# Hash logits of fourteen heads in four products instead of six, their low part in rows of its own

## The chip, the cores and the metric

The kernel runs on one core of a Trainium2 chip. The metric is the time of one execution on the device in microseconds (us): three runs of the kernel before took 732.75, 733.07 and 733.6 us, median 733.07 us.

## The reference

Two stages follow one another. First, attention with a hash mask for 2 batches x 8 heads (16 heads), 768 tokens, 64 numbers per head: q and k are multiplied by a 64 x 6 projection, the signs of the six products are a token's bucket, and a query sees only keys of its own bucket.

```python
q_bits = (np.einsum('bhsd,dk->bhsk', q, proj) > 0).astype(np.int64)
k_bits = (np.einsum('bhsd,dk->bhsk', k, proj) > 0).astype(np.int64)
mask = q_bucket[:, :, :, None] == k_bucket[:, :, None, :]
scores = np.where(mask, scale * np.matmul(q, k.transpose(0, 1, 3, 2)), -1000000000.0)
attn = softmax(scores); attn_out = np.matmul(attn, v)
```

Then the 1536 x 512 result goes through two dense layers of the form `act(x @ w_in) @ w_out` with 2048 hidden units each. The change touches the attention alone.

## The kernel before, in words

All matrix products run on TensorE in fp32r, each operand split into a rounded high part and a low part, so that one product of fp32 operands becomes two or three matmuls. Tensors named `...h` and `...l` (or `_hi`, `_lo`) are such parts. The order on every engine is the order in which the program is written (`manual_schedule`): each engine works through its own list, and waits only for data and for buffers.

The attention is a loop over 96 steps (16 heads of six query tiles of 128 rows). A step does, in the order of the string `ORDER = "ACaBbETQPR"`: A and B, three transposes each of a finished score tile into the PSUM tile `pt` (L658), of which ScalarE copies the high part `pth` (L665); C, the `clamp` of this step's scores (VectorE, L610); a and b, the low parts `ptl` (VectorE, L670); E, the exponential (ScalarE, L621); T, whatever was filed for this step in the table `todo` by `at(step, function)`; Q, the score products of the next step (L598), first `kh` with `qx`, then `kb` with `qb`, which holds the mask; P and R, the products with v (L682, L683). The PSUM pool `ps_t` has three buffers that `pt` tiles and the hash logits' tile `prep` take in turn, so the second transposes of a step take the buffer of the first transposes of the step before, and wait for that buffer's `ptl`.

Each head n is prepared about two heads ahead by `prep(n)`, which returns small functions that `start_prep` files. For n > 1: `s0` (GpSimd) rounds and subtracts q, and sends the rounded q to the upper half of `qx` by a DMA (L473 to L477); `s1` (GpSimd) does the same for k: `kh` (a `pcopy`, L109), and its low part in `qk_m` (L481). `s2` computes the hash logits: for each half of 384 tokens three matmuls, `qk_m`, `kh` and `qx` against columns of the projection's parts `pwt` (L492), all six into one PSUM tile, and right behind them `s2m`, one VectorE instruction that turns logits into mask rows `mk` (L512: greater than zero, times a constant). `s4` sends the low operands into `qb` and `kb` (L517, L518), and `s5`, one step after `s2`, sends `mk` into them in four DMAs of 32 rows (L526). `start_prep(n+1)` and `s2` of head n stand in the same step, the GpSimd part of head n+1 first. All those DMAs are issued by SyncE (SP), whose list is in program order too, with the loads of q and k (L379, L392) and the exchange of normalisers through `scr` (L647, L653).

Heads 0 and 1 are prepared at the start by other functions. In the first steps GpSimd also zeroes rows of `qb` and `kb` (`zero_rows`, step 1). Beside the preparation GpSimd has the attention outputs (`x_out` L707 to L714, `x_split` L718 and L719) and, from step 70 on, operands of the dense layers.

Of the kernel before, what the change touches and what calls it, by code (L numbers as in the profile page):

```python
# [12 lines left out]
F32 = mybir.dt.float32  # L13
# [4 lines left out]
ALU = mybir.AluOpType  # L18
# [10 lines left out]


def mask_consts():
    c = np.zeros((64, 2), np.float32)
    c[12:18, 0] = -3.0e38
    c[0:18, 1] = 1.0
    c[38:44, 0] = -3.0e38
    c[32:38, 1] = -2.0 * CBIG
    c[38:50, 1] = CBIG
    return np.concatenate([c, c])


# [1 line left out]
def lsh_attention_moe_kernel(  # L42
# [8 lines left out]
):  # L51
    nc = tc.nc
    B, H, D, S = qt.shape
    NTOK, DM = out.shape
    P = 128
    NT = S // P
# [294 lines left out]
    def attention():  # L351
        with ExitStack() as es:
# [18 lines left out]
            def load_q(n):  # L371
                b, h = head(n)
                t = nat.tile([P, S], F32, tag="qn", name="qn")
                if n == 0:
                    for f in range(2):
                        c = slice(f * HS, (f + 1) * HS)
                        nc.sync.dma_start(t[0:D, c], qt[b, h, 0:D, c])
                else:
                    nc.sync.dma_start(t[0:D], qt[b, h])  # L379
                nat_t["q", n] = t  # L380

            def load_k(n):
# [27 lines left out]
            mc = cst.tile([P, 2], F32, name="mc")  # L410
            load_q(1)
            load_k(1)
            load_v(0)
# [28 lines left out]
            pr = pp.tile([P, 2, NB], F32R, tag="p", name="pr")  # L442

            def pcol(j, o):
                w = pw[:, j, o : o + 2 * NB * (2 if o else 1)]
                return w.rearrange("p (a b) -> p a b", a=2)[:, :, 0:NB]

            def prep_w():
                nc.gpsimd.tensor_copy(mc, pc[:, 2 * NB : NC])
                pcopy(pr, pjt)  # L450
                nc.gpsimd.tensor_sub(pcol(2, 0)[0:D], rnd(pr[0:D]), pjt[0:D])
                pcopy(pcol(2, 32)[D:P], rnd(pr[D:P]))
                nc.gpsimd.tensor_sub(pcol(1, 32)[D:P], pjt[D:P], rnd(pr[D:P]))
                pcopy(pcol(1, 32)[0:D], rnd(pr[0:D]))
                nc.scalar.mul(pcol(0, 0), rnd(pr), -1.0)

            opnd = {}

            def prep(n):
# [10 lines left out]
                opnd[n] = (kh, qx, qb, kb, vv_box)  # L470

                def s0():
                    nc.gpsimd.tensor_scalar(qk_m[0:D], qn[0:D], QSCALE, 1.0, ALU.mult, ALU.mult)  # L473
                    nc.sync.dma_start(rnd(qx[D:P]), rnd(qk_m[0:D]))
                    if n > 1:
                        nc.gpsimd.tensor_scalar(qn[0:D], qn[0:D], QSCALE, 1.0, ALU.mult, ALU.mult)
                        nc.gpsimd.tensor_sub(qx[0:D], qn[0:D], rnd(qk_m[0:D]))  # L477

                def s1():
                    pcopy(kh, kn)  # L480
                    nc.gpsimd.tensor_sub(qk_m[D:P], kn[D:P], rnd(kh[D:P]))  # L481

                def second():
# [15 lines left out]

                def s2():  # L500
                    pt = ps_t.tile([P, 512], F32, tag="pt", name="prep")
                    logits(pt, 0, 64, True, False)
                    logits(pt, 1, 0, False, True)
                    mk_box.append(pt)
                    if n > 1:
                        s2m()

                def s2m():
                    pt = mk_box.pop()
                    mk = hd.tile([P, HS], F32, tag="mk", name="mk", bufs=1)  # L510
                    mk_box.append(mk)
                    nc.vector.tensor_scalar(  # L512
                        mk, pt[:, :HS], mc[:, 0:1], mc[:, 1:2], ALU.is_gt, ALU.mult
                    )

                def s4():
                    nc.sync.dma_start(rnd(qb[D:P]), rnd(qk_m[0:D]))  # L517
                    nc.sync.dma_start(rnd(kb[D:P]), rnd(qk_m[D:P]))  # L518

                def s5():  # L520
                    mk = mk_box.pop()
                    for f in range(2):
                        c = slice(f * HS, (f + 1) * HS)
                        rows = (qb, f * D), (kb, f * D + 32)
                        for t, r in rows[::-1] if f else rows:
                            nc.sync.dma_start(rnd(t[0:32, c]), mk[r : r + 32])  # L526

                def first(q1, k1):
                    cs2 = [slice(f * HS, (f + 1) * HS) for f in range(2)]
# [45 lines left out]
                return s0, s1, s2, s3, s4, s5  # L575

            NSTEP = NHD * NT
            p_t = {}
# [158 lines left out]
            NZL = 2  # L737
            PVLAG = LAG + 1
            todo = {}

            def at(step, f, *args):
                todo.setdefault(step, []).append((f, args))
# [3 lines left out]

            at(1, first_v)
            at(1, zero_rows)

            for f, st in zip(second[3:7], (2, 7, 1, 3)):  # L750
                at(st, f)

            def start_prep(n):
                b0 = NT * (n - 2)
                s0, s1, s2, s3, s4, s5 = prep(n)
                s0()
                s1()
                for f, early, late in ((s2, 8, 8), (s3, 11, 6), (s4, 6, 5), (s5, 9, 9)):
                    at(early if n == 2 else b0 + late, f)

            for u in range(NHD // 2 - 1):
                at(2 * NT * (u + 1) + XO - 3 * (u == NHD // 2 - 2), x_out, u)
# [40 lines left out]
            for i in range(NSTEP + PVLAG):  # L803
                if i == NSTEP:
                    es_s.close()
                    mps["h"] = ctx.enter_context(
                        tc.tile_pool(name="ps_h", bufs=1, space=PSUM, side="right")
                    )
                parts = iter(range(max(0, 2 * (i - NSTEP)), min(2 * (i - NSTEP) + 2, 2 * KD)))
                for part in parts:  # L810
                    r_in(0, part // KD, part % KD, part % KD + 1)
                    break
                kk = i - LAG
                tr = 0 <= kk < NSTEP
                g, j = divmod(kk, 3)
                kv = i - PVLAG
                gv, jv = divmod(kv, 3)
                for op in ORDER if i != 2 else ORDER.replace("TQ", "QT"):
                    if op == "A" and tr:
                        trp(g, 2 * j)  # L820
                    elif op == "B" and tr:
                        trp(g, 2 * j + 1)
                    elif op == "a" and tr:
                        trl(g, 2 * j)
                    elif op == "b" and tr:
                        trl(g, 2 * j + 1)
                    elif op == "C" and i < NSTEP:
                        clamp(i)
                        if i == 3:
                            second[7]()  # L830
                    elif op == "E" and i < NSTEP:
                        expo(i)
                    elif op == "Q" and i + 1 < NSTEP:
                        qk(i + 1, (0, 1) if i else (1,))
                        if i == 0:
                            keep_warm(4, 256)
                    elif op == "P" and 0 <= kv < NSTEP:
                        pv(gv, 2 * jv)
# [431 lines left out]
```

## Time and profile before

| what | value |
|---|---|
| runs | 732.75, 733.07, 733.6 us |
| span of the profiled execution | 731.7 us, 11216 instructions |
| time outside the span, against the median | 1.4 us |
| TensorE's granted clock | 0.997 of full speed on average |
| attention | from about 8 us to about 232 us of the span |
| DMA share in the attention | 0.5 to 0.7 of 16 engines |

A row of the page or of a timeline gives the engine, the line of the program, the operation, output and inputs by name, the shape, and then durations. PE is TensorE, PEld its weight loads, DVE VectorE, ACT ScalarE, POOL GpSimd, SPq the queue of DMA issues on SyncE. In a timeline the first number is the start in us, the second the time taken; a number in square brackets is how long the engine stood idle before it, and who ended that.

### The profile page before, as it was taken

The page shows a single profiled execution, that of the slowest core. Times are in us where ns is not written, and L with a number is a line of the kernel's source. Part 1 is how long each engine was busy: PE and PEld are TensorE (multiplying, and loading weights), DVE is VectorE, ACT ScalarE, POOL GpSimd, SP SyncE. Part 2 cuts the span into 40 slices and gives each one's busy share as a digit, 9 for nine tenths or more (in the row PEclk, how much of TensorE's full clock was granted, in tenths as well). Part 3 has the DMA queues.
Part 4 walks back from the last instruction along what each step waited for, and adds up shares of the span by engine and source line. Part 5 has one row for each costly group of instructions (what it writes and reads, how often), then busy time and mean ns, then how long its engine had stood idle before and what let it go on. Part 6 is the DMA issues. An engine that isn't in the chain of part 4 may idle for free.

```text
span 731.7 us, 11216 instructions
## 1 busy us (share of the span) xinstructions
PE 725.2 (99%) x3865; PEld 634.4 (87%) x3865; DVE 616.2 (84%) x1142; ACT 470.5 (64%) x965; POOL 184.9 (25%) x193
## 2 busy tenths in 40 slices
PE   8999999999999999999999999999999999999998
PEld 6999999999998788888888888888888888888886
DVE  7988889989988959888878797998699899897864
ACT  7888888888898765536546465676635556455340
POOL 6958778879894000000000000000000000000000
PEclk9999999999999999999999999999999999999999
DMA  5665565566624311122211221301302122211004
GB/s 150 167 160 146 159 179 154 155 165 166 186 74 130 98 59 58 57 72 74 87 58 58 87 84 60 116 0 59 114 2 80 65 71 73 87 58 57 1 1 172
DMA packets 25993, 69.53 MB, mean 95 GB/s; under 512 B 4464, under 2 KB 6992, under 8 KB 25936
## 3 DMA queue, kind: packets, MB, share of 16 engines
q1 hardware_dynamic: 25632, 68.62, 31.8%
q8 instruction: 30, 0.49, 0.3%
q14 instruction: 27, 0.22, 0.1%
q10 hardware_dynamic: 304, 0.20, 0.1%
HBM read 49.09 MB, written 3.19 MB: 71 GB/s over the span
## 4 chain that ended last, share of the span: by engine, by line
PE 94%; ACT 2%; DVE 2%; DMA 1%; issue 0%; ACTq 0%; DVEq 0%
PE y L929 36%; PE X L992 11%; PE s L598 9%; PE pt L658 8%; PE Y L992 8%; PE W L992 7%; PE u L683 4%; PE u L682 4%; PE h L346 4%; PE prep L492 2%; ACT p L621 1%; ACT pth L665 0%; DMA kn<-in_kt_dram 0%; DMA ul<-uh 0%; DVE gl L889 0%
## 5 line engine op out<-in xcount | busy, mean ns | idle before, releaser
L670 DVE TENSOR_TENSOR ptl<-pt,pth 128x384 fp32r<-128x384 f32 x192 | 98.1, 552 | 23.6 <-ACT pth L665 22.2
L665 ACT CAST pth<-pt 128x384 fp32r<-128x384 f32 x192 | 82.7, 482 | 28.9 <-PE pt L658 28.8
L621 ACT ACTIVATE p<-p,mn 128x768 f32<-128x768 f32 x96 | 90.9, 947 | 2.0 <-DVE p L610 1.9
L610 DVE TENSOR_SCALAR_CACHE_REDUCE p<-s 128x768 f32<-128x768 f32 x96 | 90.5, 944 | 1.0 <-PE s L598 1.0
L943 DVE TENSOR_TENSOR xq<-xq,y 128x512 f32<-128x512 f32 (+1 forms) x113 | 75.5, 678 | 13.8 <-PE y L929 13.0
L658 PE MATMUL pt<-ident,p 128*128 128x128 f32 x576 | 80.4, 274 | 0.1
L929 PE MATMUL y<-wh,gh 128*128 128x512 f32 (+1 forms) x194 | 75.4, 389 | 0.0
L929 PE MATMUL y<-wl,gh 128*128 128x512 f32 (+1 forms) x194 | 75.4, 389 | 0.0
L929 PE MATMUL y<-wh,gl 128*128 128x512 f32 (+1 forms) x194 | 75.2, 388 | 0.0
L929 PE MATMUL y<-gh,wh 128*128 128x512 f32 x192 | 75.1, 391 | 0.0
L929 PE MATMUL y<-gh,wl 128*128 128x512 f32 x192 | 75.0, 390 | 0.0
L929 PE MATMUL y<-gl,wh 128*128 128x512 f32 x192 | 74.8, 390 | 0.0
L259 ACT CAST wh<-wb 128x512 fp32r<-128x512 f32 x64 | 39.4, 619 | 54.7 <-DVE wb L246 26.2
L658 PEld LDWEIGHTS pt<-ident,p 128*128 128x128 f32 x576 | 68.4, 140 | 6.2 <-ACT p L621 0.7
L682 PE MATMUL u<-pth,vv 128*128 128x384 f32 x192 | 64.9, 338 | 0.0
L683 PE MATMUL u<-ptl,vv 128*128 128x384 f32 x192 | 64.8, 337 | 0.0
L598 PE MATMUL s<-kh,qx 128*128 128x384 f32 x192 | 56.0, 374 | 0.1
L598 PE MATMUL s<-kb,qb 128*128 128x384 f32 x192 | 50.0, 343 | 0.0
L261 DVE TENSOR_TENSOR wl<-wb,wh 128x512 fp32r<-128x512 f32 x62 | 42.2, 686 | 3.9 <-ACT wh L259 3.6
L943 DVE TENSOR_TENSOR yr<-yr,y 128x512 f32<-128x512 f32 x56 | 38.2, 683 | 7.8 <-PE y L929 6.9
L929 PEld LDWEIGHTS y<-wh,gl 128*128 128x128 f32 x194 | 36.4, 188 | 7.6
L929 PEld LDWEIGHTS y<-gl,wh 128*128 128x128 f32 x192 | 36.0, 188 | 7.9 <-DVE gl L889 0.3
(271 smaller groups left out, 1848.5 us busy)
## 6 DMA issues: line engine op xcount, KB each, us to landing
raw<-in_wt_dram SPq DMA_DIRECT2D x64, 512.0 KB
kn<-in_kt_dram SPq DMA_DIRECT2D x15, 384.0 KB
vn<-in_vt_dram SPq DMA_DIRECT2D x8, 384.0 KB
ul<-uh SPq DMA_DIRECT2D x16, 192.0 KB
rb<-scr SPq DMA_DIRECT2D x16, 192.0 KB
qn<-in_qt_dram SPq DMA_DIRECT2D x15, 192.0 KB
qx<-qk_m SPq DMA_DIRECT2D x15, 192.0 KB
qb<-qk_m SPq DMA_DIRECT2D x15, 192.0 KB
```

Source lines behind the costliest of these rows:

```text
L261: sub(lo, wf, rnd(hi))
L598: nc.tensor.matmul(s[:, f, :HS], a[:, c], bb[:, f * HS : (f + 1) * HS], start=st, stop=not st,)
L610: nc.vector.tensor_scalar(sb, s[:, :, :HS], NEG, None, ALU.min, ALU.min, accum_out=mn)
L621: nc.scalar.activation(p, p, AF.Exp, bias=mn, scale=-1.0, accum_out=z_t[n][:, t : t + 1],)
L658: nc.tensor.transpose(ptile[:, j * P : (j + 1) * P], p_t[3 * g + j][:, t * P : (t + 1) * P], ident,)
L665: nc.scalar.copy(hi, ptile[:, :HS])
L670: nc.vector.tensor_sub(lo, ptile[:, :HS], rnd(hi))
L682: nc.tensor.matmul(ut[:, :HS], vv[:, t, :], hi, start=(t == 0), stop=False)
L683: nc.tensor.matmul(ut[:, :HS], vv[:, t, :], lo, start=False, stop=(t == NT - 1))
L929: nc.tensor.matmul(y, w[:, js] if m == 0 else x[:, js], x if m == 0 else w[:, i0:i1], start=(n == 0), stop=(n == 5),)
L943: nc.vector.tensor_add(acc, acc, y)
L992: nc.tensor.matmul(bk[b], w[:, k], x, start=(first and i == 0), stop=(hook is not None and i == 2), skip_group_check=True,)
```

## The change

From the third head on (n > 1):

- `qx` is made by GpSimd on all 128 partitions (the q load brings q twice, 384 KB instead of 192 KB, as k already was), so the DMA of the rounded q goes. A new DMA sends `kh` into the lower half of `qk_m`, where the rounded q was; it waits for `kh`, GpSimd's fourth instruction of the head, where the old one waited for the first.
- The six logit matmuls become four: per half one of `qx` and one of `qk_m`, with a new weight tile `px` whose output has the logits of the high projection in rows 0 to 63 and those of its low part in rows 64 to 127. ScalarE copies the latter into `mk` right behind the matmuls.
- One step later, right behind that step's clamp, VectorE adds the former and then makes the mask rows, out of `mk` into `mk` (`mid`). `s5` follows in the same step as before, with four DMAs of 12 rows.
- `prep_x` builds `px` once, filed for step 2: on GpSimd a memset of 128 x 320 and three small copies, on SyncE two DMAs that wait for the memset and stand ahead of head 1's mask DMAs.

```diff
+            def prep_x():
+                nc.gpsimd.memset(rnd(px), 0.0)
...
+                pcopy(px[:, 0, q], rnd(pw[:, 0, 0 : 2 * NB]))
+                pcopy(px[0:D, 1, k], rnd(pw[0:D, 1, o : o + 2 * NB]))
+                pcopy(px[D:P, 1, k], rnd(pw[D:P, 2, o : o + 2 * NB]))
+                nc.sync.dma_start(rnd(px[D:P, 0, ql]), rnd(pw[0:D, 2, 0 : 2 * NB]))
+                nc.sync.dma_start(rnd(px[0:D, 1, kl]), rnd(pw[D:P, 1, o : o + 2 * NB]))
                 def s0():
+                    if n > 1:
+                        nc.gpsimd.tensor_scalar(qx, qn, QSCALE, 1.0, ALU.mult, ALU.mult)
+                        nc.gpsimd.tensor_scalar(qn[0:D], qn[0:D], QSCALE, 1.0, ALU.mult, ALU.mult)
+                        nc.gpsimd.tensor_sub(qx[0:D], qn[0:D], rnd(qx[0:D]))
+                        return
                 def s1():
                     pcopy(kh, kn)
+                    nc.sync.dma_start(rnd(qk_m[0:D]), rnd(kh[0:D]))
                     nc.gpsimd.tensor_sub(qk_m[D:P], kn[D:P], rnd(kh[D:P]))
                 def s2():
+                    if n > 1:
+                        for f in range(2):
+                            for j, x in enumerate((qx, qk_m)):
+                                nc.tensor.matmul(
+                                    pt[:, :HS],
+                                    px[:, j, 32 - 32 * f : 160 - 32 * f],
+                                    x[:, f * HS : (f + 1) * HS],
+                                    start=(f + j == 0),
+                                    stop=(f + j == 2),
+                                )
+                        mk = hd.tile([P, HS], F32, tag="mk", name="mk", bufs=1)
+                        mk_box.append(mk)
+                        nc.scalar.copy(mk[0:64], pt[64:128, :HS])
+                        return
                 def s2m():
                     if n > 1:
-                        s2m()
+                        pt, mk = mk_box
+                        del mk_box[0]
+                        nc.vector.tensor_add(mk[0:64], mk[0:64], pt[0:64, :HS])
+                        nc.vector.tensor_scalar(
+                            mk[0:64], mk[0:64], 0.0, mc[0:64, 2:3], ALU.is_gt, ALU.mult
+                        )
+                        return
                 def s5():
-                        rows = (qb, f * D), (kb, f * D + 32)
+                        rows = (qb, f * D, 0, 32), (kb, f * D + 32, 0, 32)
+                        if n > 1:
+                            rows = (qb, f * 32, 0, 12), (kb, f * 32 + 12, 6, 12)
+            at(2, prep_x)
+                mid.setdefault(9 if n == 2 else b0 + 9, []).append(s2m)
                     elif op == "C" and i < NSTEP:
                         clamp(i)
+                        for f in mid.pop(i, ()):
+                            f()
-    qt = q.transpose(0, 1, 3, 2)
+    qt = np.concatenate([q.transpose(0, 1, 3, 2)] * 2, axis=2)
```

## Rows read from the trace of the kernel before

**Rows 1.** Chain of work that ended last, 100 to 200 us: shares, then start, us, what

```profile
by line: PE s L598 31.1%; PE pt L658 29.9%; PE u L683 15.4%; PE u L682 15.4%; PE prep L492 7.4%; PE prep L640 0.9%
...
120.26 1.06 PE prep L492 x6
```

**Rows 2.** One head's stretch: us busy (instructions) of PE, PEld, DVE, ACT, POOL; clock, DMA

```profile
120.26:133.88 13.62, 13.62 (x92) 13.27 (x92) 12.11 (x27) 11.56 (x28) 8.91 (x10) 1.00 0.65 176
```

**Rows 3.** Instructions of the tile prep: count, min/median/max ns, first and last start, shapes

```profile
L492 PE MATMUL prep<-kh,pwt x30: 331/334/338, 13.2 to 202.5; 128*128 128x384 f32 x30
...
L512 DVE TENSOR_SCALAR mk<-prep,mc x15: 662/669/676, 14.3 to 203.3; 128x384 f32<-128x384 f32 x15
```

**Rows 4.** Groups by line: busy us, mean ns of one, idle before and what ended it

```profile
L670 DVE TENSOR_TENSOR ptl<-pt,pth 128x384 fp32r<-128x384 f32 x192 | 98.1, 552 | 23.6 <-ACT pth L665 22.2
...
L694 ACT COPY uh<-u 128x384 f32<-128x384 f32 x32 | 15.2, 475 | 0.0
```

**Rows 5.** Timeline from one head's logits to its first use of the mask

```profile
120.01 0.42 PE L492 MATMUL prep<-qk_m,pwt 128*128 128x384 f32 x1
...
122.06 0.95 DVE L610 TENSOR_SCALAR_CACHE_REDUCE p<-s 128x768 f32<-128x768 f32 x1
...
123.07 0.86 ACT L665 CAST pth<-pt 128x384 fp32r<-128x384 f32 x2 [1.27 <-PE pt L658]
...
123.59 1.02 DVE L670 TENSOR_TENSOR ptl<-pt,pth 128x384 fp32r<-128x384 f32 x2 [0.57 <-ACT pth L665]
...
124.61 0.82 PE L658 MATMUL pt<-ident,p 128*128 128x128 f32 x6
...
127.80 0.51 PE L598 MATMUL s<-kb,qb 128*128 128x384 f32 x2
```

**Rows 6.** VectorE instructions from SBUF to SBUF, by line

```profile
L539 DVE TENSOR_SCALAR qk_m<-qn x2: 351/352/352, 3.2 to 5.1; 64x384 fp32r<-64x384 f32 x2
...
L238 DVE TENSOR_SCALAR raw<-raw x5: 380/423/1085, 115.1 to 231.9; 128x512 uint32<-128x512 uint32 x5
...
L243 DVE SCALAR_TENSOR_TENSOR wb<-wb,raw x6: 681/693/1645, 142.3 to 235.3; 128x512 uint32<-128x512 uint32 x6
```

**Rows 7.** Timeline: one of them beside a GpSimd instruction

```profile
173.94 0.83 POOL L109 TENSOR_SCALAR kh<-kn 128x768 fp32r<-128x768 f32 x1
...
173.97 1.08 DVE L238 TENSOR_SCALAR raw<-raw 128x512 uint32<-128x512 uint32 x1
```

**Rows 8.** Timeline of GpSimd, some 3.2 us after the logits of heads 2, 8 and 15

```profile
27.51 0.84 POOL L109 TENSOR_SCALAR kh<-kn 128x768 fp32r<-128x768 f32 x1
...
109.47 1.85 POOL L707 TENSOR_TENSOR ul<-ul,uh 128x768 f32<-128x768 f32 x1
...
204.15 1.28 POOL L301 TENSOR_TENSOR t2l<-xq,t2h 128x512 fp32r<-128x512 f32 x1
```

**Rows 9.** Timelines of SyncE's DMA issues, and a GpSimd instruction that waits for one

```profile
115.58 0.29 SPq L647 DMA_DIRECT2D scr<-zt  x1
...
117.38 0.53 SPq L653 DMA_DIRECT2D rb<-scr  x1
...
122.77 1.22 SPq L526 DMA_DIRECT2D kb<-mk  x2
...
126.50 0.60 SPq L379 DMA_DIRECT2D qn<-in_qt_dram  x1
...
130.31 0.82 POOL L473 TENSOR_SCALAR qk_m<-qn 64x768 fp32r<-64x768 f32 x1 [0.97 <-DMA qn<-in_qt_dram]
```

**Rows 10.** Timelines of the start: GpSimd, then SyncE's queue, then PE

```profile
1.25 0.47 POOL L438 MEMSET wzero<- 128x448 f32 x1
...
14.53 0.82 POOL L109 TENSOR_SCALAR qb<-zero 32x768 fp32r<-32x768 f32 x1
...
15.02 0.58 SPq L526 DMA_DIRECT2D qb<-mk  x1
...
18.75 0.52 PE L598 MATMUL s<-kb,qb 128*128 128x384 f32 x2
```

More of the change, by code (lines that the diff above doesn't have):

```diff
@@ L31, in mask_consts @@
 def mask_consts():
-    c = np.zeros((64, 2), np.float32)
+    c = np.zeros((64, 3), np.float32)
     c[12:18, 0] = -3.0e38
     c[0:18, 1] = 1.0
-    c[38:44, 0] = -3.0e38
-    c[32:38, 1] = -2.0 * CBIG
-    c[38:50, 1] = CBIG
+    c[32:38, 0] = -3.0e38
+    c[32:50, 1] = CBIG
+    c[38:44, 1] = -2.0 * CBIG
+    for r in (0, 32):
+        c[r : r + 12, 2] = 1.0
+        c[r + 12 : r + 18, 2] = -2.0 * CBIG
+        c[r + 18 : r + 24, 2] = CBIG
     return np.concatenate([c, c])
@@ L53, in lsh_attention_moe_kernel @@
     B, H, D, S = qt.shape
+    D //= 2
     NTOK, DM = out.shape
@@ L378, in load_q @@
                 else:
-                    nc.sync.dma_start(t[0:D], qt[b, h])
+                    nc.sync.dma_start(t, qt[b, h])
                 nat_t["q", n] = t
@@ L409, in attention @@
             load_k(0)
-            mc = cst.tile([P, 2], F32, name="mc")
+            mc = cst.tile([P, 3], F32, name="mc")
             load_q(1)
@@ L444, in pcol @@
             def pcol(j, o):
-                w = pw[:, j, o : o + 2 * NB * (2 if o else 1)]
-                return w.rearrange("p (a b) -> p a b", a=2)[:, :, 0:NB]
+                o += NB if o else 0
+                return pw[:, j, o : o + 2 * NB].rearrange("p (a b) -> p a b", a=2)
             def prep_w():
@@ L455, in prep_w @@
                 nc.scalar.mul(pcol(0, 0), rnd(pr), -1.0)
+            px = wo[0].tile([P, DM], F32R, tag="ol1", name="px")[:, 0:320]
+            px = px.rearrange("p (a b) -> p a b", a=2)
+            def prep_x():
+                nc.gpsimd.memset(rnd(px), 0.0)
+                o = 32 + NB
+                q, k = slice(32, 32 + 2 * NB), slice(32 + 2 * NB, 32 + 4 * NB)
+                ql, kl = slice(96, 96 + 2 * NB), slice(96 + 2 * NB, 96 + 4 * NB)
+                pcopy(px[:, 0, q], rnd(pw[:, 0, 0 : 2 * NB]))
[3 more added lines that the diff above has]
+                nc.sync.dma_start(rnd(px[0:D, 1, kl]), rnd(pw[D:P, 1, o : o + 2 * NB]))
             opnd = {}
@@ L472, in s0 @@
                 def s0():
+                    if n > 1:
[3 more added lines that the diff above has]
+                        return
                     nc.gpsimd.tensor_scalar(qk_m[0:D], qn[0:D], QSCALE, 1.0, ALU.mult, ALU.mult)
                     nc.sync.dma_start(rnd(qx[D:P]), rnd(qk_m[0:D]))
-                    if n > 1:
-                        nc.gpsimd.tensor_scalar(qn[0:D], qn[0:D], QSCALE, 1.0, ALU.mult, ALU.mult)
-                        nc.gpsimd.tensor_sub(qx[0:D], qn[0:D], rnd(qk_m[0:D]))
                 def s1():
                     pcopy(kh, kn)
+                    nc.sync.dma_start(rnd(qk_m[0:D]), rnd(kh[0:D]))
                     nc.gpsimd.tensor_sub(qk_m[D:P], kn[D:P], rnd(kh[D:P]))
@@ L501, in s2, with s2m @@
                     pt = ps_t.tile([P, 512], F32, tag="pt", name="prep")
+                    mk_box.append(pt)
+                    if n > 1:
[12 more added lines that the diff above has]
+                        return
                     logits(pt, 0, 64, True, False)
                     logits(pt, 1, 0, False, True)
-                    mk_box.append(pt)
+                def s2m():
                     if n > 1:
-                        s2m()
-                def s2m():
+                        pt, mk = mk_box
[5 more added lines that the diff above has]
+                        return
                     pt = mk_box.pop()
@@ L516, in s4 @@
                 def s4():
-                    nc.sync.dma_start(rnd(qb[D:P]), rnd(qk_m[0:D]))
+                    nc.sync.dma_start(rnd(qb[D:P]), rnd(qx[D:P] if n > 1 else qk_m[0:D]))
                     nc.sync.dma_start(rnd(kb[D:P]), rnd(qk_m[D:P]))
@@ L523, in s5 @@
                         c = slice(f * HS, (f + 1) * HS)
-                        rows = (qb, f * D), (kb, f * D + 32)
-                        for t, r in rows[::-1] if f else rows:
-                            nc.sync.dma_start(rnd(t[0:32, c]), mk[r : r + 32])
+                        rows = (qb, f * D, 0, 32), (kb, f * D + 32, 0, 32)
+                        if n > 1:
+                            rows = (qb, f * 32, 0, 12), (kb, f * 32 + 12, 6, 12)
+                        for t, r, a, w in rows[::-1] if f else rows:
+                            nc.sync.dma_start(rnd(t[a : a + w, c]), mk[r : r + w])
                 def first(q1, k1):
@@ L574, in prep @@
                     return s0, lambda: nc.scalar.copy(kh, kn), second, s2, s3, s4, s5, s2m
-                return s0, s1, s2, s3, s4, s5
+                return s0, s1, s2, s3, s4, s5, s2m
             NSTEP = NHD * NT
@@ L739, in attention @@
             todo = {}
+            mid = {}
             def at(step, f, *args):
@@ L754, in start_prep @@
                 b0 = NT * (n - 2)
-                s0, s1, s2, s3, s4, s5 = prep(n)
+                s0, s1, s2, s3, s4, s5, s2m = prep(n)
                 s0()
```

## The prediction

> **What bounds the kernel now.** I read the chain of waits first. Over the middle of the attention it runs on TensorE alone: score products, transposes, products with v, and 7.4% on the hash logits, 1.06 us for a head's six [rows 1]. The table by stretch says how near the others are: in a head's 13.62 us TensorE is busy for all of it, VectorE for 12.11, ScalarE for 11.56 [rows 2]. So every TensorE instruction removed is worth its spacing, as long as nothing else gets later by more than its own slack. Those slacks I read from the timeline between a head's logits and the first use of its mask [rows 5], and from the queues of GpSimd and SyncE.
>
> **The change part by part.**
>
> *Removed from TensorE.* Six matmuls in 1.06 us are 0.177 us each. The new four have the same shape, 128x384 [rows 3], so I give them the same spacing. Two fewer in 14 heads: 28 x 0.177 = 5.0 us, all on the path. A head takes 13.27 us then.
>
> *ScalarE's copy* of 64 rows is nearest to L694, 475 ns [rows 4] (the lower end is half of a pair of `pth`, 0.43 [rows 5]). It falls where ScalarE stands idle for 1.27 us before the next `pth` [rows 5]. Nothing; with that cover gone it would cost up to 0.48 per head, 6.7 in all.
>
> *VectorE.* The old mask instruction, 0.67 [rows 3], goes. The addition reads one operand from PSUM, as L670 does: 0.55 [rows 4]. The new mask instruction goes from SBUF to SBUF; the trace has none like it with a constant per partition. Its lower end is L539, 0.35 for the same 64x384; its upper end by shape is the old one out of PSUM, 0.67; I take 0.35, the row that shares source and destination. The sum, +0.23 per head, is covered: VectorE has 1.5 us to spare in each.
>
> But its place matters. In the head at 120.01 [rows 5] the clamp would start 0.35 earlier, 121.71, and end at 122.66; the addition at 123.21; the mask at 123.56; the first `ptl` 0.55 later, 124.11. The next step's second transposes, which take that buffer, come half of 0.82 after 124.61, less 0.35: 124.67. So slack is 0.55 us.
>
> And an SBUF-to-SBUF instruction can wait for GpSimd. L238 took 1.08 where its quickest took 0.38: it started at 173.97, when GpSimd was 0.03 us into `kh`, and ended 0.28 us after that instruction's end, 174.77 [rows 7]. L243, two operands in SBUF, took 1.65 at worst, 0.69 usually [rows 6]. L670, one operand in PSUM, shows no such spread: its 192 average 0.55 [rows 4], with GpSimd busy for 8.9 of a head's 13.6 us [rows 2].
>
> The Trainium skill has this as a rule (SBUF — State Buffer, Who interferes with whom): a VectorE copy or tensor_scalar in its two-port form, and an instruction with two SBUF inputs, share a port pair with GpSimd, and whoever issues first holds it for the whole instruction. The trace agrees, with 1.08 against 0.38. By the rule the new mask instruction waits whenever GpSimd is at work; by L539 alone, 0.35 whatever GpSimd does, the time would be 730.5.
>
> So the new mask instruction waits w, the rest of the GpSimd instruction in flight some 3.2 us after the logits' start, and TensorE loses w - 0.55 where that is positive. With GpSimd as it stands today, w over the 14 heads runs from 0.5 (head 2: `kh` from 27.51) through 1.75 (head 8, logits from 106.4: L707 from 109.47) to 0.55 (head 15: until 205.43) [rows 8]; over all 14 the excess adds up to about 7 us. GpSimd will stand later relative to TensorE, though (below). Spread evenly over a head with GpSimd's durations (1.85 two or three times, 1.28 twice, 0.84 three times [rows 8]) the excess is 0.2 per head, 3 us. Bounds 0 and 8; I take 4.5.
>
> *Mask DMAs.* The mask is ready at 123.56 + w, not 122.1. The third of the four DMAs, for which the second half of the first product waits, starts 1.2 later (0.6 apiece [rows 9]), and lands 1.8 after that, by the 3 KB transfer that released L653 1.8 after its issue (upper end 3.8: the 192 KB q load, 126.50 to 130.31 [rows 9]). So 126.6 + w, needed at 127.80 + 0.17 - 0.35 = 127.6, plus whatever TensorE has lost. Covered by 0.45 at least; but SyncE must be free.
>
> *SyncE's new order.* The DMA of `kh` waits for GpSimd's fourth instruction of the next head where the old waited for its first, and the mask DMAs stand behind it. GpSimd starts a head when q has landed, and already waited 0.97 us for it [rows 9]. Now q is 384 KB, 1.1 us more at 176 GB/s [rows 2], and its issue stands 1.4 us later behind later mask DMAs. So `kh` ends 2 us later against TensorE, about when the mask is ready. A round (four mask issues 2.4; one or two issues of the exchange, 0.6 each; q's issue and landing 4.9; four GpSimd instructions 4.5 with their gaps; the issue for `kh` 0.5) is 12.9 to 13.5 us against a period of 13.27: it nearly closes on itself. Mostly hidden; 0.6 us for heads whose loads stand behind a weight load. Bounds 0 and 6.
>
> *GpSimd per head* does the same five instructions; 128 partitions cost what 64 do (`kh`, 128x768: 0.84; L473, 64x768: 0.82 [rows 8, 9]).
>
> *The start.* `prep_x` follows `zero_rows`, which ends at 15.35. Its memset, by columns of the 448-wide one's 0.47, ends near 15.75 [rows 10]. Then SyncE's two DMAs, at 0.55 to 0.6, and only at 16.9 head 1's mask DMAs, which started at 15.02. Their third lands 16.9 + 1.2 + 1.8 = 19.9 against 18.92 needed [rows 10]: 1.0 lost. The three copies hold GpSimd up too (memset and copies about 1.4); `kh` of head 2 holds SyncE, q of head 3 is issued late, and head 2's mask stands behind `kh` of head 3: I make that 0.7 more. Together 1.8; bounds 0 (the DMAs go ahead earlier than I think) and 3.
>
> *Dense layers.* They begin when attention ends and wait on nothing of this; shift one for one.
>
> **Sum.** -5.0 + 4.5 + 0.6 + 1.8 = +1.9 us. The profiled execution's span of 731.7 becomes 733.6; with the 1.4 us around it 735.0, against a median of 733.07.
>
> **The rivals.**
>
> *The mask instruction does not wait* (a constant per partition may put it in another form, or GpSimd happens to stand in short instructions or gaps then). Then -5.0 + 0.6 + 1.8 = -2.6: 730.5. For it: L539's two ran 0.35 each, and GpSimd is idle for a third of a head's stretch [rows 2]. Against: L238 waited. It decides from w below 0.55.
>
> *Everything is hidden*, the start too: -5.0, 728.1. For it: TensorE's stream shows no wait today. Against: the start's sum is short by a whole microsecond.
>
> *SyncE's round is the bound.* If q lands a microsecond later than I think, `kh` holds up the mask DMAs every other head, 0.8 us times seven: 5.6 more, 740.6. For it: the 12.9 to 13.5. Against: 12-row DMAs move less, 72 KB a head instead of 192.
>
> **How the numbers follow.** Forecast 0.45, no wait 0.27, all hidden 0.12, SyncE's round 0.10, the rest in between, 0.06. 0.2% is 1.5 us, about what a measurement can tell from no change. Faster by more: most of the second (0.22), the third (0.12), a little of the first: 0.36. Slower by more: 0.28 of the first, all of the fourth, 0.01: 0.39. Same 0.25. The forecast's own range is 732.5 to 738.0; over all cases 728.6 to 739.8, which leaves out about half of the third and most of the fourth.
>
> **What would show it.** Right: L492 with 28 fewer matmuls; the mask instruction with a median well above 0.35 and a maximum near 2, ending just behind a GpSimd instruction's end; TensorE waiting at L658 for `ptl` in the step after the logits, and near 18.75 us for head 1's mask; heads of 13.3 to 14.5 us. Wrong: the mask instruction at 0.35 to 0.4 throughout; heads of 13.27 us from end to end; no wait at 18.75; or TensorE waiting for mask DMAs in most heads, which is the round.

## The result: slower by 1.3%, and the profile after

The changed kernel took 742.85 us (median of four runs, 740.8 to 744.44) against 733.2 for the kernel before: ratio 1.0129, 95% interval 1.0115 to 1.0142. A second set (`e23_after_again`) gave 743.84, 1.0144 [1.013, 1.0158]. The forecast of 735.0 had the sign and lay 8 us too low, outside its range. The span grew from 731.7 to 741.2: 8.5 us by the first matmul of the dense layers' product `y` (238.70 before, 247.24 after, from the timelines), 1.0 behind TensorE's last matmul.

First TensorE's waits, from the table of groups of the profile after (busy us, mean ns | idle before, and what ended it):

```profile
L702 PE MATMUL pt<-ident,p 128*128 128x128 f32 x576 | 80.6, 273 | 3.6 <-DVE ptl L714 3.6
L702 PEld LDWEIGHTS pt<-ident,p 128*128 128x128 f32 x576 | 68.4, 140 | 9.8 <-DVE ptl L714 5.4
...
L642 PE MATMUL s<-kb,qb 128*128 128x384 f32 x192 | 54.1, 352 | 4.7 <-DMA kb<-mk 3.6
...
L642 PEld LDWEIGHTS s<-kb,qb 128*128 128x128 f32 x192 | 34.6, 187 | 10.9 <-DMA kb<-mk 5.5
```

Two waits are new, one for `ptl` and one for the mask rows (`kb<-mk`). By the waits view the second ends 14 idle times of the weight loads:

```profile
PEld s L642 <- DMA kb<-mk: 5.5, 14, 0.6
```

The instructions around the mask (count, min/median/max ns, first and last start), which answer to [rows 3, 4]:

```profile
L570 SPq DMA_DIRECT2D qb<-mk x30: 578/714/883, 17.2 to 217.0; - x30
L570 SPq DMA_DIRECT2D kb<-mk x30: 588/719/782, 17.8 to 216.2; - x30
L537 ACT COPY mk<-prep x14: 475/477/482, 27.9 to 212.6; 64x384 f32<-64x384 f32 x14
L546 DVE TENSOR_TENSOR mk<-mk,prep x14: 540/541/545, 28.7 to 213.1; 64x384 f32<-64x384 f32 x14
L547 DVE TENSOR_SCALAR mk<-mk,mc x14: 532/997/2085, 29.2 to 213.7; 64x384 f32<-64x384 f32 x14
```

The copy and the addition have the forecast's durations. The mask instruction L547 spreads as forecast. The DMAs are the surprise: 0.71 to 0.72 us to issue one of 12 rows, where one of 32 rows took 0.566 and 0.582 before.

Two heads' stretches, to be held against [rows 2] (PE, PEld, DVE, ACT, POOL busy; clock, DMA share, GB/s):

```profile
68.63:83.34 14.71, 13.67 (x93) 12.88 (x91) 13.77 (x28) 12.26 (x28) 8.93 (x10) 1.00 0.59 164
111.34:124.82 13.48, 13.45 (x93) 12.90 (x91) 12.93 (x29) 12.50 (x29) 12.75 (x13) 1.00 0.69 184
```

Heads now take 13.48 to 14.71 us, 14.2 on average from 26.11 on, where TensorE had 13.62 before and 13.27 was to be had. What holds them alternates. In one kind of head the mask instruction meets GpSimd's subtraction L503 (timeline):

```profile
71.78 2.08 DVE L547 TENSOR_SCALAR mk<-mk,mc 64x384 f32<-64x384 f32 x1
71.82 1.83 POOL L503 TENSOR_TENSOR qk_m<-kn,kh 64x768 fp32r<-64x768 f32 x1
...
73.79 1.01 DVE L714 TENSOR_TENSOR ptl<-pt,pth 128x384 fp32r<-128x384 f32 x2
73.90 0.81 SPq L570 DMA_DIRECT2D qb<-mk  x1
74.39 0.31 PEld L702 LDWEIGHTS pt<-ident,p 128*128 128x128 f32 x3 [1.26 <-DVE ptl L714]
74.39 0.55 PE L702 MATMUL pt<-ident,p 128*128 128x128 f32 x3 [1.02 <-DVE ptl L714]
74.76 1.55 SPq L570 DMA_DIRECT2D kb<-mk  x2
...
77.65 0.19 PEld L642 LDWEIGHTS s<-kb,qb 128*128 128x128 f32 x1 [0.34 <-DMA kb<-mk]
```

L547 ends 0.21 after GpSimd's instruction, `ptl` stands behind it, the transposes behind `ptl`: the forecast's mechanism. And even then, with TensorE 1.02 late already, it waits for the mask once more at 77.65. In the other kind of head the mask instruction is held for less, but SyncE stands at `kh`:

```profile
133.94 0.58 SPq L384 DMA_DIRECT2D qn<-in_qt_dram  x1
...
138.28 0.83 POOL L493 TENSOR_SCALAR qx<-qn 128x768 fp32r<-128x768 f32 x1 [3.79 <-PE s L642]
...
141.92 0.83 POOL L114 TENSOR_SCALAR kh<-kn 128x768 fp32r<-128x768 f32 x1
142.05 0.92 DVE L547 TENSOR_SCALAR mk<-mk,mc 64x384 f32<-64x384 f32 x1
142.78 0.46 SPq L502 DMA_DIRECT2D qk_m<-kh  x1
...
143.37 0.79 SPq L570 DMA_DIRECT2D qb<-mk  x1
...
144.20 1.53 SPq L570 DMA_DIRECT2D kb<-mk  x2
...
147.07 0.19 PEld L642 LDWEIGHTS s<-kb,qb 128*128 128x128 f32 x1 [0.39 <-DMA kb<-mk]
```

The mask is ready at 142.97, its first DMA starts 0.40 later, behind that of `kh`. And `kh` comes when it does because of the q load: L493, the first GpSimd instruction of the next head, ends an idle time of 3.79 us. The profile puts that wait to a score product, but the last landing record of the q load, issued at 133.94, is at 138.15; in all seven heads of this kind (2, 4, 6, 8, 10, 12, 14) L493 starts 0.1 to 0.2 us behind that record. SyncE's waits for `kh` are 25.8 us in 13 (none of them a loss in itself). And the start [rows 10]:

```profile
15.63 0.36 POOL L466 MEMSET px<- 128x320 f32 x1
...
16.52 0.60 SPq L474 DMA_DIRECT2D px<-pwt  x1
...
17.22 0.58 SPq L570 DMA_DIRECT2D qb<-mk  x1
...
19.88 0.98 PE L642 MATMUL s<-kb,qb 128*128 128x384 f32 x2 [1.41 <-DMA kb<-mk]
```

I summed, matmul by matmul, how far each start lay behind the usual spacing of its kind before (the median by kind of neighbours), up to that first `y`: 4.6 us at the transposes that wait for `ptl`, 5.5 at the mask rows after head 2, 1.9 at head 1's mask, 1.2 at head 2's, 0.8 scattered; with the 5.0 saved, +9.0 against the +8.5 measured. Of the 5.5 some 4.3 lie in heads 4, 6, 8, 10, 12 and 14, where the mask DMAs start 0.4 to 1.3 us behind the mask, and 1.1 in the seven others, where they start at once but the mask itself is late.

### The profile page after: what moved, and what is told of

Its sections match the earlier page's. It is cut to its first block, busy times and chain, and to the rows that moved or that the text cites. A ratio compares the mean times of both kernels' runs of the same rounds, so it can differ in the third digit from the quotient of the medians.

```text
span 741.2 us, 11170 instructions
## 1 busy us (share of the span) xinstructions
PE 726.4 (98%) x3837; PEld 628.9 (85%) x3837; DVE 628.7 (85%) x1156; ACT 479.7 (65%) x979; POOL 186.5 (25%) x197
## 4 chain that ended last, share of the span: by engine, by line
PE 82%; DVE 6%; DMA 6%; SPq 2%; ACT 2%; issue 1%; POOL 0%; DVEq 0%
PE y L978 35%; PE X L1041 11%; PE Y L1041 7%; PE W L1041 7%; PE s L642 6%; PE pt L702 5%; PE h L351 4%; PE u L727 2%; PE u L726 2%; DVE mk L547 2%; DMA raw<-in_wt_dram 2%; DMA kb<-mk 2%; DVE ptl L714 1%; DMA kb<-qk_m 1%; SPq L570 1%
## 5 line engine op out<-in xcount | busy, mean ns | idle before, releaser
L642 PE MATMUL s<-kb,qb 128*128 128x384 f32 x192 | 54.1, 352 | 4.7 <-DMA kb<-mk 3.6
L642 PEld LDWEIGHTS s<-kb,qb 128*128 128x128 f32 x192 | 34.6, 187 | 10.9 <-DMA kb<-mk 5.5
```

Source lines behind the costliest of these rows:

```text
L642: nc.tensor.matmul(s[:, f, :HS], a[:, c], bb[:, f * HS : (f + 1) * HS], start=st, stop=not st,)
```

## The experiments

Theory A was that SyncE's new order costs the mask waits: the mask DMAs stand behind the transfer of `kh`. Rival B: the mask comes late whatever stands ahead of it, by the copy, the addition and slower issues. Later a sharper form: no head has any cover left.

**What the saved matmuls are worth** (`e5_four_only`): the kernel before with

```diff
                     for j, x in enumerate((qk_m, kh, qx)):
+                        if two and j == 1:
+                            continue
```

and `two = n > 1`.

> The kernel before with the two products of kh left out of the hash logits from the third head on, so four matmuls where there were six; nothing else differs (the hash of these heads is then not the reference's). It measures the term of the saved matmuls alone: 28 x 0.177 = 5.0 us, 728.0 to 728.5, if TensorE is the bound in these stretches. If other waits take the room, 730 to 733.

729.04 us, 0.9939 [0.9926, 0.9952]: 4.2 us. Its heads take 13.27 as forecast, two of them more (13.33, 13.81). So 4 to 5 us were to be had and the change gave back 13 to 14.

**The parts on the kernel before.** `e3_prepx_only` adds `prep_x` alone, its result unused.

```diff
+            at(2, prep_x)
```

> The kernel before, with prep_x added (it builds the new weight tile, which nothing uses here). Theory (SyncE issues head 1's mask DMAs 2 us late and TensorE waits 1.5 to 2 us for them, about 3 us with what follows in head 2): 734.5 to 736 us, with a wait of TensorE near 19 us of the span. Rival (the start is hidden): 733.2 us, no wait there.

735.35, 1.0029 [1.0018, 1.004], as expected: 1.2 us between heads 1 and 2, the other heads at 13.55 to 13.63. Some 0.7 lie behind the last matmul, as 1.0 do in the changed kernel; no view says why.

`e4_moves_only` moves q and k as the change does (q loaded twice, `qx` whole on GpSimd, the DMA of `kh`) and keeps six products, masks and 32-row DMAs (the hash of heads 2 to 15 then works on other numbers).

```diff
                     pcopy(kh, kn)
+                    nc.sync.dma_start(rnd(qk_m[0:D]), rnd(kh[0:D]))
```

> The kernel before, with only the movement of q and k as in the changed kernel: q loaded twice, qx made on 128 partitions, the DMA of kh in place of that of the rounded q. Still six logit products, and the mask made right behind them out of PSUM; the products have another operand in half of qk_m, so heads 2 to 15 are hashed by other numbers than the reference's. Theory (SyncE behind kh bites only because the mask is 1.4 us and more later in the changed kernel; here the mask has that slack): 733 to 735 us, with at most a wait in head 2. Rival (the later kh and the doubled q load cost by themselves): 737 us or more, with TensorE waiting for mask DMAs in many heads.

733.91, 1.001 [1.0, 1.0019]. Head 2 takes 14.38: its mask DMAs start 3.3 us behind the mask, and TensorE loses 0.7. The other heads take 13.61 to 13.62. So SyncE's new order alone costs 0.7 in one head and nothing in the rest of a kernel whose mask is early. That already spoke against theory A, with a limit: here `kh` itself comes earlier, after head 2 0.3 to 2.1 us behind the start of the products (2.3 to 4.6 in the changed kernel), and it holds the mask DMAs up in three more heads only (3, 12 and 14, by 0.6 to 1.3, and by 0.1 in head 8), where nothing is lost.

**The wait for GpSimd** (`e1_psum`): the addition writes where the logits are, and the mask instruction reads there.

```diff
-nc.vector.tensor_add(mk[0:64], mk[0:64], pt[0:64, :HS])
+nc.vector.tensor_add(pt[0:64, :HS], mk[0:64], pt[0:64, :HS])
...
-    mk[0:64], mk[0:64], 0.0, mc[0:64, 2:3], ALU.is_gt, ALU.mult
+    mk[0:64], pt[0:64, :HS], 0.0, mc[0:64, 2:3], ALU.is_gt, ALU.mult
```

> The changed kernel, but VectorE's addition writes into PSUM and the mask instruction reads from there, so that no instruction of the hash goes from SBUF to SBUF. Theory (the mask instruction waits for GpSimd): it takes 0.67 us in all 14 heads instead of 0.5 to 2.1, TensorE's waits for ptl (4.8 us over the attention) go, some waits for the mask DMAs stay in the heads where SyncE stands behind kh: 737 to 739 us. Rival (SyncE's order and the late mask are all of it): TensorE's waits move from ptl to the mask DMAs and the time stays within 2 us of 742.9. Rival (the mask instruction is slow by itself, whatever GpSimd does): its time still varies from head to head.

740.65, 1.0104 [1.0059, 1.0149], four runs between 737 and 745. Its mask instruction, by tile, and what TensorE waits for:

```profile
L547 DVE TENSOR_SCALAR mk<-prep,mc x14: 609/609/610, 29.2 to 209.7; 64x384 f32<-64x384 f32 x14
```

```profile
PE s L642 <- DMA kb<-mk: 4.2, 8, 1.1
```

From PSUM all 14 take 0.61 whatever GpSimd does; out of SBUF it was 0.53 to 2.09. The rule that the forecast weighed (the Trainium skill, SBUF — State Buffer, Who interferes with whom) holds here, a constant per partition included. The waits for `ptl` are gone (0.2 us at most), those for the mask stay, and the median gains 2 where 4.6 went, though with four runs that far apart its size is uncertain. In the profiled execution (738.72 us) the mask waits after head 2 are 7.0 us by the sum over the matmuls, not 5.5: one wait had covered part of the other.

**SyncE's order.** My first try (`e2_kh_later`) filed the DMA of `kh` two steps later, which put it not only behind the masks but behind the loads.

```diff
-                    nc.sync.dma_start(rnd(qk_m[0:D]), rnd(kh[0:D]))
...
+                    at(b0 + 4, s1d)
```

> The changed kernel, but the DMA of kh into qk_m is filed two steps later (heads 3 to 15), so that on SyncE the mask DMAs of the head before stand ahead of it and not behind. Theory (SyncE's order costs some 4 us, in every other head and in head 2, the rest is the mask instruction's wait and the start): 738 to 740 us, with TensorE's waits for ptl still there. Rival (the mask is late only because VectorE makes it late): 742 to 744 us. Rival (SyncE's order is all of the loss): 731 to 735 us.

763.83, 1.0407 [1.038, 1.0433]: a bad test, since it moved too much. TensorE waits for `kh` at the products:

```profile
PE prep L530 <- DMA qk_m<-kh: 21.1, 9, 5.2
```

The 192 KB stand behind q, k and sometimes a 512 KB weight load, and land too late. The better test is `e11_kh_behind_masks`, one step earlier, between masks and loads:

```diff
-                    at(b0 + 4, s1d)
+                    at(b0 + 3, s1d)
```

> The changed kernel, with the 192 KB transfer of kh into qk_m filed one step later than its copy, so that it stands on SyncE behind the four mask DMAs of the head before it and still ahead of the q and k loads. Everything else is as in the changed kernel. Theory A (SyncE's order: kh, whose copy on GpSimd takes half a head in every other head, holds the mask DMAs up, and TensorE waits for the mask rows): the some 4 us of waits of TensorE for qb<-mk and kb<-mk fall to below 1.5, the waits for ptl stay at about 4.8, 738.5 to 739.5. Rival B (the mask rows come late because their DMAs are issued late and slowly whatever stands ahead of them: the addition, the mask and four issues of 0.7 us): the mask waits stay above 3 us, 742 to 743.

739.06, 1.0089 [1.0062, 1.0116], six runs between 736.6 and 743.6. In the median what theory A said, but not in the way it said: by the sum over the matmuls of the profiled execution (736.6 us) TensorE still waits 4.8 us for the mask after head 2 (5.5 in the changed kernel), most of it in four heads (0.6 to 1.1 us at a time; in heads 12 and 14 behind another neighbour on SyncE, told below), and once 0.7 for `kb<-qk_m`; it is the waits for `ptl` that are nearly gone (0.8), since GpSimd meets the mask instruction elsewhere (it takes 0.41 to 1.23). TensorE's waits by the waits view, head 1 among them:

```profile
PE s L644 <- DMA kb<-mk: 3.1, 5, 1.4
```

**The issue of the DMAs** (`e12_rows32`): 32 rows again.

```diff
-rows = (qb, f * 32, 0, 12), (kb, f * 32 + 12, 6, 12)
+rows = (qb, f * 32, 0, 32), (kb, f * 32, 0, 32)
```

> The changed kernel with mask DMAs of 32 rows as in the kernel before, in place of 12 (the rows that they fetch are partly others, so the masks of heads 2 to 15 are not the reference's). Rival B (the issue of a 12-row DMA costs 0.71 us against 0.57, so the pair that is waited for lands later): the issues go back to 0.57 to 0.58, and of the mask waits some 2 us go, 740.5 to 741.5. Theory A (SyncE's order): the issues get shorter, the waits for the masks lose only 0.1 to 0.3 us in each of the seven heads where they occur, 741.5 to 742.5.

737.82, 1.0065 [1.0046, 1.0084]: 5 us, more than either expected, with `kh` still ahead. The issues are back at 0.58 to 0.59. The trace kept is that of the slowest of the six runs (740.88): there TensorE waits 4.1 us for masks after head 2 and 5.0 for `ptl`, so it does not show where the rest of the 5 us went.

**The mask earlier** (`e15_step7_only`): products, addition, mask and DMAs one step (2.2 us) earlier, `kh` still ahead of the mask DMAs.

```diff
-for f, early, late in ((s2, 8, 8), (s3, 11, 6), (s4, 6, 5), (s5, 9, 9)):
+for f, early, late in ((s2, 8, 7), (s3, 11, 6), (s4, 6, 5), (s5, 9, 8)):
```

> The changed kernel with the hash products, the addition and the mask of a head all filed one attention step (2.2 us) earlier; kh's transfer keeps its place ahead of the mask DMAs on SyncE. Theory A (the mask DMAs are late because SyncE holds them behind kh's transfer, which waits for GpSimd's copy): the mask is ready 2.2 us earlier, but its DMAs still start behind kh, 3 to 5 us after the head's products; the mask waits of TensorE stay at 2 to 4 us, 739 to 742. Rival B (the mask itself is late, by the copy, the addition and the issue of 12-row DMAs): 2.2 us is more than any wait seen, they all go, 737 to 738.5 with the waits for ptl left.

737.08, 1.0055 [1.0042, 1.0068]: rival B's number, in part by luck, since the waits for `ptl` that it left in fell too (from 4.8 to 1.8 by the sum over the matmuls), and the new place costs some 0.16 a head (below). The mask waits that are left are at heads 1 and 2, whose steps did not move:

```profile
PE s L642 <- DMA kb<-mk: 1.7, 2, 1.4
```

Theory A as the whole cause falls: in eleven of the heads after head 2 the mask DMAs still start 0.4 to 1.7 us behind the mask, after `kh`, and hurt nobody.

**Three edits together** (`e13_three`): `e1_psum`, `e11_kh_behind_masks`, and the GpSimd part of `prep_x` in step 1 ahead of `first_v`, its DMAs behind head 1's `qb` and `kb`.

```diff
+            at(1, prep_x)
             at(1, first_v)
             at(1, zero_rows)
-            at(2, prep_x)
...
+            at(1, prep_xd)
```

> The changed kernel with three edits at once: the addition writes into PSUM and the mask instruction reads PSUM, the kh transfer is filed behind the mask DMAs and ahead of the loads, and the GpSimd part of prep_x stands in step 1 ahead of first_v and zero_rows with its two DMAs behind those of head 1's qk_m. If the three waits are separate (ptl 4.8, masks 4, start 2 to 3), they go together and leave 742.9 - 4.8 - 3.5 - 1.5 = 733, 731.5 to 734.5, near the kernel before; the 5 us of matmuls saved would then be eaten by what is left of the start and of the waits. If the waits are one behind the other, so that taking one away brings out the next, 736 to 740.

735.0, 1.0027 [1.0018, 1.0036]. The start is mended (11.72 between heads 1 and 2; 11.63 before), ten of the other heads take 13.24 to 13.77, three (8, 12 and 14) 14.4 to 15.5. In these three SyncE stands at another neighbour, `rb<-scr`, the second half of the exchange of normalisers, which waits for the first half to land; the mask DMAs start 2.3, 0.6 and 1.7 us behind the mask. Head 8 (timeline):

```profile
107.75 0.61 DVE L553 TENSOR_SCALAR mk<-prep,mc 64x384 f32<-64x384 f32 x1
...
110.10 0.47 SPq L703 DMA_DIRECT2D rb<-scr  x1
110.66 0.81 SPq L576 DMA_DIRECT2D qb<-mk  x1
```

With 32-row DMAs on top (`e19_three_rows32`: this and the diff of `e12_rows32`):

> The kernel of the three edits with mask DMAs of 32 rows in place of 12 (the rows fetched are partly others, so the masks of heads 2 to 15 are not the reference's). With SyncE's order already put right, what is left of the mask waits (4.2 us in the profiled execution) is by rival B the issue of the 12-row DMAs: 3 us go, 731.5 to 732.5. By theory A the issue is worth 0.4 us on the third of four DMAs in heads that have that slack: 734 to 735.

733.37, 1.0004 [0.9994, 1.0013]: 1.6 us, between the two.

**Is there any cover?** In a quiet head of `e13_three` the chain reads so:

```profile
77.59 0.42 PE L534 MATMUL prep<-qx,px 128*128 128x384 f32 x1
...
80.73 0.61 DVE L553 TENSOR_SCALAR mk<-prep,mc 64x384 f32<-64x384 f32 x1
...
81.37 0.81 SPq L576 DMA_DIRECT2D qb<-mk  x1
82.23 1.53 SPq L576 DMA_DIRECT2D kb<-mk  x2
...
85.01 0.54 PE L648 MATMUL s<-kb,qb 128*128 128x384 f32 x2
```

From the products' start: mask at 3.75, third DMA at 5.46, landed at 7.48 by the trace's records of landings, second half of the product due at 7.42 + 0.17. That leaves 0.1 us. In all seven heads that take 13.24 to 13.26 it is 0.03 to 0.13. In the kernel before, the same records give the first matmul of that product 1.3 to 2.5 us after the third landing. To weigh it, one more DMA ahead of the masks in either kernel, in the one before as `e20_before_dup`, in the three edits as `e21_three_dup`:

```diff
+                        if n > 1 and f == 0:
+                            nc.sync.dma_start(dum, mk[0:12])
```

> The kernel before, with one more DMA from the third head on: 12 rows of the mask, to a scratch tensor, ahead of the four mask DMAs on SyncE. It makes each mask DMA some 0.7 us later. In the trace of before the last of the three needed mask transfers lands 1.3 to 2.5 us ahead of the matmul that needs it, so nothing should be lost: 732.9 to 733.6. If mask DMAs cost time in themselves (the queue, contention), 14 x 0.7 = 9.8 us at most, 743.

> The kernel of the three edits with the same extra DMA ahead of its mask DMAs. If its masks land with no slack in every head (theory: the chain copy, addition, mask, 12-row issues has used up all of it), each of 13 or 14 heads pays 0.7 to 0.8 us: 735.0 + 9.5 to 10.5 = 744 to 746. If the waits that are left there come from collisions in a few heads and the others have the microsecond that the prediction gave them, 735 to 737.

733.07, 0.9998 [0.999, 1.0007] for the first: nothing. 740.9, 1.0105 [1.0087, 1.0124] for the second, 5.9 us on top of 735.0. Neither case that I had expected: I had the delay too large, since to a tensor in HBM the DMA issues in 0.33. What it delayed was paid almost in full, in every quiet head (timeline, and the stretch from products to products):

```profile
97.49 0.32 SPq L576 DMA_DIRECT2D dum<-mk  x1
97.86 0.81 SPq L578 DMA_DIRECT2D qb<-mk  x1
98.72 1.54 SPq L578 DMA_DIRECT2D kb<-mk  x2
...
101.61 0.19 PEld L651 LDWEIGHTS s<-kb,qb 128*128 128x128 f32 x1 [0.47 <-DMA kb<-mk]
```

```profile
93.71:107.28 13.57, 13.42 (x93) 12.86 (x90) 12.40 (x28) 12.11 (x28) 8.88 (x9) 1.00 0.58 151
```

The masks start 0.37 later and the head takes 13.57 instead of 13.25, 0.32 more.

**Versions with the mask earlier.** `e14_all_step7` is the three edits with the diff of `e15_step7_only`.

> The kernel of the three edits (addition in PSUM, kh's transfer behind the mask DMAs, GpSimd part of prep_x first) with products, addition and mask one step earlier as well. Theory A and rival B agree here: nothing holds the mask DMAs, they start 2.2 us earlier, and the 4.2 us of mask waits left in the kernel of the three edits go. What is left is 5.0 us of matmuls saved less the start: 729 to 731, faster than the kernel before. If it is not, a third thing (GpSimd, or the landings) holds it: 733 to 735.

731.99, 0.9985 [0.9976, 0.9994] in eleven runs: faster than both kernels, by 0.15%, 1.5% below the changed one. The mask waits are gone but for one of 0.3, yet a head takes

```profile
89.24:102.67 13.43, 13.43 (x92) 12.87 (x91) 12.42 (x28) 11.96 (x29) 8.63 (x10) 1.00 0.62 156
```

13.43, not 13.25: the transposes at 93.48 take 1.01 instead of 0.82. They need the newest exponential, which ends at 93.7, and by the waits view it ends 15 idle times of their weight loads, one in nearly every head:

```profile
PEld pt L708 <- ACT p L671: 3.3, 15, 0.3
```

`e17_psum_px_step6` has `e1_psum` and the earlier `prep_x`, and goes two steps earlier, with `kh` where the change put it.

```diff
+for f, early, late in ((s2, 8, 6), (s3, 11, 6), (s4, 6, 5), (s5, 9, 7)):
```

> The changed kernel with the addition in PSUM, the GpSimd part of prep_x first, and products, addition and mask two steps (4.4 us) earlier. The mask DMAs then stand ahead of the next head's kh transfer on SyncE without moving that. If SyncE's order and the lateness of the mask are all that costs, 729 to 731, as for the one step with kh's transfer moved. If the products now come too early for kh's own transfer or for GpSimd's subtraction into qk_m, TensorE waits for them at the products: 732 to 740.

735.62, 1.0033 [1.0021, 1.0044], in the band expected for products that come too early, but not for that reason: most heads take 13.46 to 13.49, and single waits are left (2.2 us for head 2's mask, 1.3 for an exponential). `e22_end7` is the three edits with the products at the end of the step before, 1.4 us earlier.

```diff
+                for f in tail.pop(i, ()):
+                    f()
```

> The kernel of the three edits with the four products moved from the middle of an attention step to the end of the step before it (1.4 us earlier), copy, addition, mask and DMAs accordingly. If lateness of the mask is what is left, all mask waits go and a head takes 13.25 us: 735.0 - 4 to 5 = 730 to 731. If the place ahead of the step's transposes costs TensorE 0.18 us a head as the whole step earlier did, 732 to 733.

733.8, 1.0012 [1.0004, 1.0021]. TensorE waits for no mask DMA, but a head takes 13.56 to 13.59: ahead of a step's transposes the products cost 0.3 more than in its middle, and the weight loads of transposes wait for the exponential 16 times, 4.8 us. `e23_after_again` is the changed kernel itself.

> The changed kernel itself again, beside the others on one chip: 741 to 744 as before, with a spread of some 3 us between its runs, since each run's small delays on SyncE and GpSimd fall elsewhere and none is covered.

743.84 (741.82 to 744.75). The spread of the runs goes roughly with the cover: 1.7 to 2.7 us for the versions of the change with the mask early, 2.6 to 8 for those without, in 4 to 11 runs each.

## Why the prediction was wrong, step by step

- **Removed matmuls, -5.0.** Right: 13.27 us a head when nothing else is in the way, 4.2 us of time.
- **Copy on ScalarE, addition, at nothing.** Durations right to 0.01. That they cost nothing in themselves was right for the engines; that they lie on the way of the mask was counted, and is the step below.
- **The mask instruction, +4.5.** Right: 4.6, six heads of fourteen paid. The mechanism and the slack of 0.55 hold: in the head above 2.08 - 0.35 - 0.55 = 1.18, and by the sum over the matmuls TensorE lost 1.19. That the total came out so close is partly luck, since 4.5 was picked between 3 and 7.
- **The failed step is "Mask DMAs": "Covered by 0.45 at least".** It put TensorE's waits for the mask at nothing; 5.5 us after head 2 went there. The working gave 1.05 us of cover in a head without a wait, of which a wait of the mask instruction takes up to 0.55. Measured without a wait it is 0.1 in the quiet head above, whose mask comes 0.2 later out of PSUM, so 0.3 out of SBUF. The parts: third DMA 1.7 after the first, not 1.2, since I took the issue of a 32-row DMA for one of 12 rows (0.5); landing 2.0 us after its issue, not 1.8 (0.2). So the cover was negative in every head where the mask instruction waited, and where `kh` stood ahead.
- **"Mostly hidden; 0.6" for SyncE's order** followed from that cover. Of the 5.5 us 4.3 lie in the six heads where `kh` stands ahead. `kh` does end about when the mask is ready, as the text had it, and delays its DMAs by 0.4 to 1.3 in every second head; but where there is cover the same hold costs nothing (`e15_step7_only`, three heads of `e4_moves_only`). And with `kh` out of the way (`e11_kh_behind_masks`) 4.8 of the 5.5 are still there, 2.5 of them in heads 12 and 14, where `rb<-scr` now does the holding: a hold is a price only without cover.
- **The start, +1.8.** Undersized: 1.9 for head 1 and 1.2 for head 2, 3.1 in all. The mechanism was right; the mask DMAs began at 17.22, not 16.9, and the matmul that needs the third started at 20.4, not 19.9. Head 1's products also came 0.45 earlier here than in the trace of before; in `e1_psum`, `e3_prepx_only` and `e12_rows32`, where they came when they did before, the same wait is 1.3 to 1.4. Head 2's share is not `prep_x`'s: `e3_prepx_only` does not have it, and `e4_moves_only`, without `prep_x`, has 0.7 of it, behind `kh` of head 3.
- **Rivals.** SyncE's round (740.6, chance 0.10) named the place, the pattern and nearly the size. Its sign, "TensorE waiting for mask DMAs in most heads", is in the profile; `kh` does hold the mask DMAs up in every second head, seven times, by 0.4 to 1.3 us (in head 14 `rb<-scr` has a part in it), and the mask waits of these seven heads come to 5.5 us, against its 5.6. Its premise, a q load a microsecond later than forecast, is not what the trace shows: `kh` hangs on the q load in all seven, but it ends about with the mask, as the forecast had it: in five heads 0.2 us ahead of the mask, whose instruction waited for that very copy, and only in two (2 and 12) 0.7 behind it. What it did not name is the missing cover, which turns a hold of 0.4 into a wait. The other two are refuted by L547's 0.53 to 2.09.
- **Outside the sum.** From the last matmul to the end it is 3.1 us in the kernel before and in the three here without `prep_x`, and 0.4 to 1.0 more in all kernels with it but one (`e21_three_dup`). Not explained.

## What to carry to other kernels

Before a chain of small steps is made longer, write down its cover from first start to first use, and take every duration in it from a row of the same shape: here an issue of 12 rows was priced as one of 32, and with it 0.7 us of a cover of 1.05 was not there. It was not all: with issues of 32 rows (`e12_rows32`) the changed kernel was still slower than the one before. Cover that is used up does not show as one large wait: any delay elsewhere, a wait of VectorE for GpSimd, a neighbour in the queue (`kh`, and behind it `rb<-scr`), is then paid nearly in full, and the runs begin to scatter. When such waits show, moving the chain earlier (`e15_step7_only`, one number in a table) tells lateness from order better than reordering the queue; it also moves the chain's other meetings, so read the waits and not only the time.

## What the runs showed that was not expected

- A DMA between two places of SBUF took longer to issue with 12 rows (0.714 and 0.719 us) than with 32 (0.566 and 0.582; again 0.588 and 0.583 in `e12_rows32`), though it moves 18 KB and not 48. To HBM, 12 rows issued in 0.30 to 0.33. The 12-row transfers leave 13 landing records each, one about 1.2 us after the issue began and twelve around 2.0; the 32-row ones leave 16. The Trainium skill (DMA: Bandwidth & Descriptors, Why a DMA increments its semaphore by 16 and not by 1) has the count: the number of DMA engines is the largest up to 16 that divides the rows, and the issuer adds the rest at once. The trace agrees with twelve and one; the longer issue the page does not give for this chip.
- In `e2_kh_later`, behind a wait of 5.2 us, TensorE's granted clock was 0.50 for 2 us and 0.77 over six more, the level of 1.2 GHz and a mixture of the two:

```profile
183.90:185.90 2.00, 1.99 (x6) 2.00 (x7) 0.00 (x0) 0.48 (x1) 1.92 (x2) 0.50 0.23 54
186.00:192.00 6.00, 6.00 (x33) 5.88 (x32) 4.89 (x11) 3.40 (x8) 3.40 (x4) 0.77 0.05 10
```

The products then come 0.32 us apart, not 0.177. None of the changed kernel's waits, 1.4 us at most, did that: its clock stayed at 1.00 at 74.3 and at 20.0.
